# Fourier mixing and a two-layer network on one core: the last transform's copies with their two loops exchanged

## The chip, the cores and the metric

The kernel runs on one core of a Trainium2 chip. The metric is device time in microseconds of one execution. TensorE is written PE in the profile (its weight loads PEld), VectorE DVE, ScalarE ACT, GpSimd POOL; SP issues DMAs only.

## The reference

Eight sequences of 3008 rows with 256 channels go through a Fourier transform along the sequence, a complex 256 x 256 layer, a soft threshold, and the inverse transform. The 24064 rows that come out go through a network with 2048 hidden channels.

```python
X = np.fft.rfft(x, axis=1)                      # x: (8, 3008, 256)
Yr = Xr @ w_r - Xi @ w_i + b_r
Yi = Xr @ w_i + Xi @ w_r + b_i
Y  = soft(Yr, 0.01) + 1j * soft(Yi, 0.01)       # sign(v) * max(|v| - 0.01, 0)
y  = np.fft.irfft(Y, n=3008, axis=1).reshape(24064, 256)
h  = y @ w_in                                   # 256 -> 2048
out = (s * np.maximum(h, 0) ** 2 + b) @ w_out   # 2048 -> 256
```

## The kernel before

The transform of length 3008 is split into 94 x 32, with row n = 32 n1 + n2 (n1 below 94, n2 below 32), so that each part is a matmul with a small table. For every batch there are four steps. The first (`s1_units`) multiplies by the table of length 94. The second and third (`s23_units`) do the transform of length 32, the complex layer, the threshold and the transform back, with a turn through DRAM on either side. The last (`s4_units`) multiplies by the table `C_t` of length 94 and gives `yt`.

`yt` holds the rows of a batch for the network: 128 partitions are 128 channels, `DC` = 2 blocks of channels, then 96 x 32 two-byte values (n1 outside, n2 inside), so that n2 is contiguous and one n1 is a row of 64 bytes. The network reads `yt` as the moving side of its first matmuls, sixteen n1 with all n2 at a time (512 rows).

The last step goes over fourteen groups: n2 in steps of five (0, 5, ..., 25, then two from 30 on), and for each of these the two blocks of channels. For a group, PE does one matmul for each n2 with 94 columns, one behind the other in a bank of PSUM (pool `psf`, two banks), so that in the bank n2 is outside and n1 inside, four bytes a value. Then `leave_bank` (its copy is at L297) puts down one copy of 470 values (188 for the last groups) per partition that turns the order round and writes fp16 into `yt`.

Whether a copy runs on ACT or DVE, and in which place, is not decided while the program is built: `later` collects such pieces, and the table `TURNS` gives every piece its engine and its place in the order, written out by hand. The order on PE is in the program too: for each block of 128 hidden channels (a slot) come two matmuls of the first layer into one half of a double bank (`psh`, two of them), some matmuls of the second layer into `psa`, and a unit of the transform of a later batch. The fourteen units of the last step take the last slots before the batch's own tiles begin (for batch 1, sixteen slots around that point). A batch's first tile needs all its copies; for batch 1, whose tiles go over half the n2 at a time, the copies of that half.

Other work on ACT and DVE in these slots: relu (L1122 on ACT, L1124 on DVE) and square (L1133, L1135) of the hidden values, sums of squares for a product with seven instead of eight block products (L1276), and the sums that leave `psa` (L1234, L1333). POOL copies a batch's last 14 n1 from `yt` (L1036) once all copies are done, and issues DMAs behind that (x at L353, an adding DMA at L1290). Matmuls all appear at L234. Batch 0 has a last step of its own in `first_batch`, with groups of four n2.

Of the kernel before, what the change touches and what calls it, by code (L numbers as in the profile page):

```python
# [16 lines left out]
N1 = 94  # L17
# [140 lines left out]
def kernel(  # L158
# [73 lines left out]
    def matmul(out, lhs, rhs, **how):  # L232
        pump()
        return nc.tensor.matmul(out, lhs, rhs, **how)  # L234
# [37 lines left out]
    def need(ops):  # L272
        assert all(op.gone for op in ops)

    def later(emit, cost, needs=(), frees=None):

        op = SimpleNamespace(emit=emit, cost=cost, needs=list(needs), gone=False)
        if frees is not None:
            reads[id(frees)].append(op)
        if pe["on"]:  # L280
            pieces.append(op)
            return op
        e = min(cost)
        if "act" in cost:
            e = "act" if act_first(cost["act"], cost["dve"]) else "dve"
            work(e, cost[e])
        begin(op, e)
        return op
# [6 lines left out]
    def leave_bank(dst, bank, src, cols, needs=()):  # L295
        def emit(e):
            (nc.scalar.copy if e == "act" else nc.vector.tensor_copy)(out=dst, in_=src)  # L297

        return later(emit, copy_cost(cols), needs=needs, frees=bank)
# [30 lines left out]
    def one_bank():  # L330
        return track("psf", 2, fpool.tile([P, 512], F32, name="psf", tag="psf"))
# [672 lines left out]
    def s4_units(b):  # L1004

        groups = []
        for lo in range(0, N2, 5):
            for ec in range(DC):
                groups.append((lo, min(5, N2 - lo), ec))

        def unit(g):
            n2, w, ec = groups[g]
            if g == 0:
                yts[b] = ypool.tile([P, DC, 96, N2], F16, name="yt", tag="yt")
            yt = yts[b]
            ps = one_bank()
            need([half_loads[(b, h)] for h in {n2 // HW, (n2 + w - 1) // HW}])
            for j in range(w):
                h, k = divmod(n2 + j, HW)
                matmul(  # L1020
                    ps[:, j * N1 : (j + 1) * N1],
                    vs[(b, h)][:, k, ec * P : (ec + 1) * P], C_t[:, 0:N1],
                    start=True, stop=True,
                )

            done = leave_bank(
                yt[:, ec, 0:N1, n2 : n2 + w], ps,
                ps[:, 0 : w * N1].rearrange("p (j n) -> p n j", n=N1), w * N1,
            )
            y_ops[b].append((n2, w, done))  # L1030
            if g == len(groups) - 1 and b >= 2:
                pr, half = divmod(b, 2)
                if half == 0:
                    tails[pr] = tpool.tile([P, DC, 2, 14, N2], F16, name="tail", tag="tail")
                tail_copies[b] = later(
                    lambda e: nc.gpsimd.tensor_copy(  # L1036
                        out=tails[pr][:, :, half], in_=yt[:, :, 80:94, :]
                    ),
                    {"pool": 1.8}, needs=[op for _, _, op in y_ops[b]],
                )  # L1040

        return [lambda g=g: unit(g) for g in range(len(groups))]


# [419 lines left out]
    for b in range(2, B):  # L1464
        s0, s1, s2 = mark[b - 2], mark[b - 1], mark[b]
        p = s1 - s0
# [4 lines left out]
        p = s2 - s1  # L1471
# [57 lines left out]
```

## Time and profile before

| | |
|---|---|
| median of 3 runs | 835.43 us (834.75 to 836.34) |
| the profiled execution | 835.52 us |
| its span | 833.7 us |
| granted TensorE clock | 1.00 |
| last-step copies of batches 1 to 7 | 56 on ACT, 42 on DVE |
| stages of these copies, first copy to last | 93.67 us in seven pieces |

The profile is of one execution. A group row such as those in the prediction gives line, engine, operation, what is written and read, shape and count, then the busy time in us, the mean of one in ns, and the idle time of the engine before them with what ended it. A row of the timeline gives start and duration in us, and in brackets the engine's idle time before it. Neighbouring instructions of an engine overlap by about 0.1 us, so durations on a full engine add up to a little more than the time.

### The profile page before, as it was taken

What the parts mean: (1) busy time and instruction counts of PE and PEld (TensorE: products, weight loads), DVE (VectorE), ACT (ScalarE), POOL (GpSimd) and SP (SyncE); (2) the same over time, 40 slices, a digit from 0 to 9 for tenths busy, and PEclk for the clock granted to TensorE, in tenths of its full rate; (3) what the DMA queues carried; (4) which work ended last, traced back from release to release, by engine and by line L of the source; (5) the groups of instructions that cost most, each with busy time, mean ns of one, the idle gap of its engine ahead of it and who ended that gap; (6) DMA issues with size and microseconds to landing.
All of it is one profiled execution on the core that took longest, in us unless ns stands there. A gap on an engine that the chain in (4) does not pass through costs nothing.

```text
span 833.7 us, 19076 instructions
## 1 busy us (share of the span) xinstructions
PE 818.9 (98%) x7662; PEld 598.5 (72%) x7662; DVE 736.8 (88%) x1192; ACT 702.2 (84%) x874; POOL 83.4 (10%) x112
## 2 busy tenths in 40 slices
PE   7999999999999999999999999999999999999997
PEld 6857777777677767777677766777667777767765
DVE  5988989997898999998899979999989989889984
ACT  5989889989798889888889988897879987878774
POOL 4630000100011000110001100110001000001000
PEclk9999999999999999999999999999999999999999
DMA  8963546664547367454656545654566333513222
GB/s 202 182 170 82 120 138 171 131 129 123 173 114 166 85 176 188 108 118 128 176 141 161 112 124 150 150 130 116 129 177 149 72 92 96 140 45 77 74 49 77
DMA packets 114929, 107.14 MB, mean 129 GB/s; under 512 B 11036, under 2 KB 99104, under 8 KB 113496
## 3 DMA queue, kind: packets, MB, share of 16 engines
q1 hardware_dynamic: 100760, 80.55, 33.2%
q0 software_dynamic: 14080, 25.37, 18.5%
q8 instruction: 60, 0.98, 0.5%
q14 instruction: 29, 0.24, 0.1%
HBM read 53.52 MB, written 46.66 MB: 120 GB/s over the span
## 4 chain that ended last, share of the span: by engine, by line
PE 83%; DVE 8%; DMA 5%; ACT 2%; issue 1%; POOL 0%; SPq 0%; DVEq 0%; ACTq 0%; POOLq 0%
PE psh L234 34%; PE psa L234 31%; PE psf L234 17%; DMA ring<-ring 2%; DMA gt<-gt 2%; DVE rt L1124 1%; DMA x<-in_x_dram 1%; PE psm L234 1%; DVE gt L1135 1%; ACT rt L1122 1%; DVE u L297 1%; DVE yt L297 1%; DVE gt L1276 1%; DVE ring L934 0%; POOL x L370 0%
## 5 line engine op out<-in xcount | busy, mean ns | idle before, releaser
L234 PEld LDWEIGHTS <-gt 128*128 128x128 f16 (+1 forms) x3696 | 305.1, 101 | 168.9 <-DMA gt<-gt 1.1
L234 PE MATMUL psh<-yt,w_in 128*128 128x512 f16 (+1 forms) x1344 | 397.2, 378 | 1.5 <-ACT u L297 0.8
L1122 ACT ACTIVATE rt<-psh 128x1024 f32<-128x1024 f32 (+2 forms) x310 | 311.4, 1006 | 63.1 <-PE psh L234 55.7
L234 PE MATMUL psa<-w_out_t,gt 128*128 128x256 f16 (+3 forms) x2448 | 310.1, 253 | 0.7 <-DMA gt<-gt 0.6
L1133 ACT ACTIVATE gt<-rt 128x1024 f16<-128x1024 f32 (+2 forms) x254 | 261.6, 1041 | 11.4 <-DVE rt L1124 8.6
L1135 DVE TENSOR_TENSOR gt<-rt 128x1024 f16<-128x1024 f32 (+2 forms) x130 | 154.3, 1194 | 7.7 <-ACT rt L1122 7.0
L234 PEld LDWEIGHTS <-w_in 128*128 128x128 f16 x1536 | 136.3, 98 | 25.2 <-issue 3.2
L1124 DVE TENSOR_SCALAR rt<-psh 128x1024 f32<-128x1024 f32 (+2 forms) x74 | 88.2, 1193 | 19.9 <-PE psh L234 17.5
L1290 POOL DMA_DIRECT2D gt<-gt x42 | 38.1, 907 | 505.5 <-DVE gt L1276 231.6
L234 PE MATMUL psa<-T_s,gt 128*128 128x128 f16 (+1 forms) x944 | 79.6, 219 | 0.3 <-DVE zz L1333 0.3
L890 DVE TENSOR_TENSOR ring<-psf,s 128x512 f16<-128x512 f32 x84 | 57.6, 686 | 19.9 <-PE psf L234 11.1
L234 PE MATMUL psh<-tail,w_in 128*128 128x512 f16 (+1 forms) x192 | 52.1, 353 | 0.0
L234 PEld LDWEIGHTS <-xf 128*128 128x128 f16 x504 | 47.1, 98 | 4.9 <-DVE xf L850 0.5
L234 PE MATMUL psf<-W_g,xf 128*128 128x256 f16 x336 | 50.4, 273 | 0.0
L297 ACT CAST yt<-psf 128x470 f16<-128x470 f32 (+2 forms) x60 | 37.1, 646 | 4.4 <-PE psf L234 4.2
L1234 DVE SCALAR_TENSOR_TENSOR ost<-psa,s_bc,bias_bc 128x512 f32<-128x512 f32 (+2 forms) x51 | 36.9, 723 | 3.0 <-PE psa L234 2.9
L234 PE MATMUL psf<-x,A_t 94*96 94x512 f16 x102 | 38.9, 382 | 0.3 <-DVE u L297 0.2
L297 ACT CAST xf<-psf 128x512 f16<-128x512 f32 x52 | 30.3, 585 | 10.1 <-PE psf L234 9.9
L1333 DVE SCALAR_TENSOR_TENSOR ost<-psa,s_bc,zz 128x256 f32<-128x256 f32 (+1 forms) x80 | 36.6, 477 | 1.6 <-PE psa L234 0.8
L234 PE MATMUL psf<-C_t,vs 96*128 96x94 f16 (+1 forms) x484 | 37.7, 205 | 0.3 <-ACT yt L297 0.3
L297 ACT CAST u<-psf 96x512 f16<-96x512 f32 x54 | 31.0, 578 | 6.7 <-PE psf L234 5.4
L297 ACT CAST v<-psf 128x512 f16<-128x512 f32 x49 | 28.6, 583 | 9.3 <-PE psf L234 9.1
(121 smaller groups left out, 890.8 us busy)
## 6 DMA issues: line engine op xcount, KB each, us to landing
out_dram<-ost SPq DMA_DIRECT2D x65, 256.0 KB
ud<-u SPq DMA_DIRECT2D x56, 192.0 KB
us<-ud SPq DMA_DIRECT2D x28, 384.0 KB
vd<-v SPq DMA_DIRECT2D x42, 256.0 KB
vs<-vd SPq DMA_DIRECT2D x14, 768.0 KB
x<-in_x_dram POOLq DMA_DIRECT2D x28, 376.0 KB, 6.4
gt<-gt POOLq DMA_DIRECT2D x38, 256.0 KB, 4.0
ring<-ring SPq DMA_DIRECT2D x120, 64.0 KB
```

The lines of the kernel that those rows point to most:

```text
L234: return nc.tensor.matmul(out, lhs, rhs, **how)
L297: (nc.scalar.copy if e == "act" else nc.vector.tensor_copy)(out=dst, in_=src)
L890: lambda e: nc.vector.tensor_tensor(out=ring[0][:, i % 4], in0=ps, in1=hold[i // 2][:, i % 2].unsqueeze(1).to_broadcast([P, 2, D]), op=ALU ...
L1122: nc.scalar.activation(out=rt, in_=ps[:, :, 0:w], func=AF.Relu)
L1124: nc.vector.tensor_scalar(out=rt, in0=ps[:, :, 0:w], scalar1=0.0, scalar2=None, op0=ALU.max)
L1133: nc.scalar.activation(out=gt, in_=rr, func=AF.Square)
L1135: nc.vector.tensor_tensor(out=gt, in0=rr, in1=rr, op=ALU.mult)
L1234: nc.vector.scalar_tensor_tensor(out=osts[number % 3][0:size, 0:k], in0=ps[0:size, 0:k], scalar=s_bc[0:size], in1=bias_bc[0:size].unsqueez ...
L1276: nc.vector.tensor_tensor(out=out, in0=a, in1=b, op=op)
L1290: nc.gpsimd.dma_start(out=a12, in_=a11, accum_op=ALU.add)
L1333: nc.vector.scalar_tensor_tensor(out=out, in0=of, scalar=s_bc[0:size], in1=other, op0=ALU.mult, op1=ALU.add)
```

## The change

The copies of `s4_units` write the same values from the same bank to the same places, in the other order: n2 outside, n1 inside. The source is then read in the order in which it lies, and the destination gets one two-byte value in each 64-byte row before the next.

```diff
             done = leave_bank(
-                yt[:, ec, 0:N1, n2 : n2 + w], ps,
-                ps[:, 0 : w * N1].rearrange("p (j n) -> p n j", n=N1), w * N1,
+                yt[:, ec, 0:N1, n2 : n2 + w].rearrange("p n j -> p j n"), ps,
+                ps[:, 0 : w * N1].rearrange("p (j n) -> p j n", n=N1), w * N1,
             )
```

Batch 0's copies, the table of turns and all other lines are as before.

## The prediction

> **What bounds the kernel now.** I read the busy shares first, then the chain that ended last.
>
> ```profile
> PE 818.9 (98%) x7662; PEld 598.5 (72%) x7662; DVE 736.8 (88%) x1192; ACT 702.2 (84%) x874; POOL 83.4 (10%) x112
> PE 83%; DVE 8%; DMA 5%; ACT 2%; issue 1%; POOL 0%; SPq 0%; DVEq 0%; ACTq 0%; POOLq 0%
> ```
>
> TensorE (PE) sets the time. The copies run on ScalarE (ACT) and VectorE (DVE), which have slack on the whole. What counts is their slack in the seven stages in which the copies run: batches 1 to 7, from first copy to last. The busy time by stage is the second view (columns: window, its length, busy time of PE, PEld, DVE, ACT, POOL, then clock, DMA share and GB/s):
>
> ```profile
> 230.63:243.60 12.97, 12.97 (x181) 10.20 (x179) 12.14 (x22) 12.26 (x18) 1.76 (x2) 1.00 0.59 153
> 718.50:731.20 12.70, 12.69 (x186) 10.69 (x185) 11.11 (x19) 12.67 (x20) 1.71 (x2) 1.00 0.31 65
> sum 93.67, PE 93.29 PEld 73.73 DVE 88.93 ACT 89.79 POOL 12.07; mean PE 13.33 PEld 10.53 DVE 12.70 ACT 12.83 POOL 1.72
> ```
>
> In these 93.67 us PE idles 0.38, ACT 3.88 and DVE 4.74: half a microsecond per stage and engine. Three engines are full at once, so more work on ACT or DVE is not hidden here.
>
> The groups by shape, for the price of a copy today:
>
> ```profile
> L297 ACT CAST yt<-psf 128x470 f16<-128x470 f32 x52 | 34.0, 683 | 2.9 <-PE psf L234 2.7
> L297 DVE CAST yt<-psf 128x470 f16<-128x470 f32 x32 | 22.4, 704 | 3.4 <-PE psf L234 3.4
> L297 ACT CAST yt<-psf 128x188 f16<-128x188 f32 x4 | 1.2, 321 | 0.0
> L297 DVE CAST yt<-psf 128x188 f16<-128x188 f32 x10 | 3.2, 347 | 1.1 <-PE psf L234 1.0
> L297 ACT CAST v<-psf 128x512 f16<-128x512 f32 x49 | 28.6, 583 | 9.3 <-PE psf L234 9.1
> L297 DVE CAST v<-psf 128x512 f16<-128x512 f32 x35 | 23.8, 681 | 2.0 <-PE psf L234 1.9
> ```
>
> The v rows read and write in order. With the 128x1024 rows at L1122 and L1124 (1022 and 1219 ns), a value costs (1022 - 583)/512 = 0.857 ns on ACT and 1.051 on DVE, over a fixed 144 and 143 ns. At that rate 470 values take 547 (ACT) and 637 ns (DVE), and 188 take 305 and 340.
>
> The yt copies lie above that, and single instructions show where. In batch 2 the first copies start at n2 = 0, 0, 5, 5, 10, ...:
>
> ```profile
> 230.63 0.55 ACT L297 CAST yt<-psf 128x470 f16<-128x470 f32 x1
> 232.07 0.83 ACT L297 CAST yt<-psf 128x470 f16<-128x470 f32 x1
> 239.12 0.75 ACT L297 CAST yt<-psf 128x470 f16<-128x470 f32 x1 [0.17 <-PE psf L234]
> ```
> ```profile
> 231.06 0.65 DVE L297 CAST yt<-psf 128x470 f16<-128x470 f32 x1 [0.40 <-PE psf L234]
> 236.17 0.74 DVE L297 CAST yt<-psf 128x470 f16<-128x470 f32 x1
> 240.19 0.64 DVE L297 CAST yt<-psf 128x470 f16<-128x470 f32 x1
> ```
>
> The means over the seven stages, by starting n2, read instruction by instruction: at 0, 10 and 25, ACT 585 and DVE 645 ns; at 15 and 20, ACT 762 and DVE 738; at 5, ACT 828 and DVE 818. PSUM is read the same way in all of them. What differs is the place of the written run: five two-byte values, ten bytes, in a 64-byte row of yt. Runs at 0, 10 and 25 lie within one aligned block of 16 bytes; at 15 and 20 one value is cut off from four; at 5 the cut is 3 + 2. So the write side has a price by block, and the strided PSUM read has next to none (645 against 637). After the change every value is written 64 bytes from the last, a block each.
>
> **The change part by part.** No instruction is added, moved or reordered: the order of all engines stays, with 52 + 4 copies on ACT and 32 + 10 on DVE in these stages (470 and 188 values). Batch 0 keeps its own copies. Only the price changes, and no row shows single values at a 64-byte step. The bounds:
> - Nothing: 547/305 ns on ACT, 637/340 on DVE (470/188 values). ACT loses 7.1 us in all, DVE 2.2.
> - The pair price. The 188-value copies write two values per 64-byte row, at (321 - 144)/94 = 1.88 ns a row on ACT and (347 - 143)/94 = 2.17 on DVE. If a single value needs as long as such a pair: ACT 144 + 470 x 1.88 = 1.03 us (0.50 for 188), DVE 1.16 (0.55).
> - The price of the cut-off value. The runs cut 1 + 4 pay (762 - 585)/94 = 1.88 ns extra on ACT and (738 - 645)/94 = 0.99 on DVE per lone value. On all values: ACT 585 + 470 x 1.88 = 1.47 us (0.68), DVE 1.11 (0.53).
> - The price of the 3 + 2 cut (243/94 = 2.59 and 173/94 = 1.84 ns) on every value: ACT 1.80 us (0.81), DVE 1.51 (0.69).
>
> The pair rows have the right step, the cut rows the right number of values. On DVE both say the same: I take 1.13 us (0.54). On ACT I take the middle, 1.25 (0.59).
>
> The Trainium skill, "Vector Engine (DVE) Microarchitecture Reference", section "5.2 Measured stream behaviour on trn2", speaks against this change: a destination that hops with every element is given as 1.71 ns an element for far hops and 2.50 for a 96-byte step, against 1.05 for runs of two or more. An estimate by that page is 0.95 to 1.32 us for 470 values on DVE, and with the same prices on ACT some 6 to 28 us for the kernel by the same sum as below. "SBUF — State Buffer", "Specifications (TRN2)", says that a 16-byte line needs two hits for full bandwidth; the 3 + 2 runs have two or more on each line and still cost 818 ns, so the trace agrees with the line and not with the count.
>
> Now the path. Stage by stage, the extra work of an engine is the new price less what its copies take now. What hides it is the engine's idle time in the stage, and the lead of the last copy over the first matmul that reads it. Where units and copies end in batch 2:
>
> ```profile
> 242.62 0.25 PE L234 MATMUL psf<-C_t,vs 96*128 96x94 f16 x2
> 244.30 0.59 PE L234 MATMUL psh<-yt,w_in 128*128 128x512 f16 x2
> ```
>
> The last copy ends at 243.59 and the matmul at 244.30 waits for all copies of its batch: a lead of 0.71. For batches 3 to 7 the leads are 0.95, 0.56, 0.70, 0.54 and 0.62. Batch 1 reads its second half later; there I allow 1.0, the time between two units on the two psf banks. Extra on ACT at 1.25 us, batches 1 to 7: 4.3, 4.0, 5.1, 3.9, 5.4, 3.0, 4.9 (sum 30.6); on DVE 2.3, 2.5, 1.8, 2.5, 1.5, 3.3, 1.7 (15.6). ACT is the later engine in all but batch 6, where DVE has eight of the fourteen copies. Idle on ACT: 0.20, 0.71, 0.34, 0.65, 1.32, 0.63, 0.03; on DVE in batch 6: 0.14. Take idle and lead off the later engine: 3.1 + 2.6 + 3.8 + 2.7 + 3.4 + 2.6 + 4.2 = 22.3 us. PE has nothing to catch this up with: 0.38 us idle.
>
> What queues behind: on ACT the relus at L1122 and squares at L1133, whose two psh banks hold up PE's next pair; on DVE the sums at L1276 and the out additions, which free psa. On POOL the tail copy waits for the last yt copy (26.8 us in all today), and behind it the gt additions and x loads. They shift with PE, and I count nothing more for them.
>
> The profiled execution took 835.52 us (span 833.7), the median of the runs is 835.43. So 835.4 + 22.3 = 857.7 us.
>
> **The rivals.**
> - *Pair price on both engines.* For it: the 188-value rows have this very step and run at full rate. Against: a lone value may not go like a pair. The same sum with ACT 1.03 and DVE 1.16: 1.5 + 1.2 + 1.8 + 1.3 + 1.4 + 2.8 + 2.2 = 12.2 us, giving 847.6.
> - *Cut-off price on every value.* For it: lone values exist in the trace and cost that. The sum is 33.4 us, giving 868.8; with the 3 + 2 price 51.7, giving 887.1. Against: those runs go to the neighbouring block, and ours never do.
> - *The hop is free* (ends at no change or faster). If the cost lies in cutting a run, not in the block, then writes at 64 bytes are free, as for pairs, and the cuts are gone: ACT 7.1 us and DVE 2.2 less. PE can take up only its 0.38 us of idle time in the stages, and perhaps as much at their ends: 834.7 to 835.1. It decides while an ACT copy stays under about 0.84 us (3.88 idle + 5.08 lead over 56 copies is 0.16 above 683) and a DVE copy under about 0.94. The Trainium skill's "Advanced Engine Details and Errata", "PSUM Cachelines", wants every two consecutive elements adjacent, by which the read in order would gain; the trace shows 8 ns of 645 to be had. That nothing changes because the pattern is folded back is in this case too: the order of the loops in the built instructions does change (94x5 to 5x94).
>
> **How the numbers follow.** Middle price 0.32, pair price 0.27, cut-off price 0.20, 3 + 2 price or worse 0.08, free or unchanged 0.13. The range leaves out the free case and the 3 + 2 price: from 842, the pair case with some more lead, to 872, the cut-off case with a little on top. A difference under 0.2% (1.7 us) can't be told from none. The free case is mostly within it: 0.10 same and 0.03 faster. The rest, 0.87, is slower.
>
> **What would show it.** Right: the 470-value copies near 1.25 us on ACT and 1.13 on DVE, alike for all starting n2; stages 2 to 4 us longer, with PE idle before psh matmuls, on yt or on ACT's relus; nothing else changed. Wrong: copies at about 0.55 and 0.64 us (free), or ACT copies above 1.45; or copies as forecast but stages longer by less than 1 us, so that leads are larger than I counted; or stages longer by ACT and DVE together, so that the two delays add.

## The result, and the profile after

The changed kernel takes 921.93 us (median; 920.77 to 923.95) against 835.8 us in the same comparison: a ratio of 1.1035, 95% interval 1.1012 to 1.1058, or +86 us. Forecast were +22 us and a range that ended at 872. The direction and the place were right; the price of a copy was not.

The busy time of the page, then three of the seven stages of the copies (the second, the sixth and the seventh, first copy to last) and the sum of all seven:

```profile
PE 845.2 (92%) x7662; PEld 612.9 (67%) x7662; DVE 790.6 (86%) x1192; ACT 782.6 (85%) x874; POOL 83.3 (9%) x112
243.40:268.90 25.50, 18.04 (x189) 12.98 (x187) 20.64 (x21) 23.61 (x19) 1.76 (x2) 0.87 0.29 75
683.00:707.30 24.30, 15.70 (x193) 11.19 (x190) 24.23 (x24) 21.96 (x18) 1.77 (x2) 1.00 0.36 92
790.50:817.90 27.40, 17.44 (x194) 13.42 (x192) 16.97 (x20) 27.36 (x22) 1.71 (x2) 0.88 0.14 30
sum 182.30, PE 121.22 PEld 88.52 DVE 144.15 ACT 173.40 POOL 12.06; mean PE 17.32 PEld 12.65 DVE 20.59 ACT 24.77 POOL 1.72
```

The seven stages grew from 93.67 to 182.30 us, by 88.6. The rest of the span went from 740.0 to 737.8. So the whole loss lies where the copies are, and there ACT is now busy for 173.4 of 182.3 us while PE is not. The groups of the copies:

```profile
L297 ACT CAST yt<-psf 128x470 f16<-128x470 f32 x52 | 114.2, 2338 | 6.4 <-PE psf L234 6.4
L297 DVE CAST yt<-psf 128x470 f16<-128x470 f32 x32 | 71.4, 2256 | 26.9 <-PE psf L234 26.9
L297 ACT CAST yt<-psf 128x188 f16<-128x188 f32 x4 | 3.8, 1080 | 1.8 <-PE psf L234 1.8
L297 DVE CAST yt<-psf 128x188 f16<-128x188 f32 x10 | 10.0, 1074 | 6.3 <-PE psf L234 6.3
L297 ACT CAST v<-psf 128x512 f16<-128x512 f32 x49 | 28.5, 582 | 8.2 <-PE psf L234 7.9
L297 DVE CAST v<-psf 128x512 f16<-128x512 f32 x35 | 23.9, 682 | 2.0 <-PE psf L234 1.8
```

A copy of 470 values went from 0.68 to 2.34 us on ACT and from 0.70 to 2.26 on DVE. The v copies, which write in order, are as before. The two engines, whose rates differ (0.857 and 1.051 ns a value), now pay nearly the same: (2256 - 1074)/282 = 4.2 ns a value on DVE and 4.5 on ACT. So what limits them now is not the engine's own rate.

How PE comes to wait, in the waits of the whole kernel (waiting line, who ends the wait, total us, times, longest) and in the timeline of batch 2, ACT first, then one line of PE:

```profile
PE psf L234 <- ACT yt L297: 48.7, 43, 1.9
PE psf L234 <- DVE yt L297: 10.5, 13, 1.6
```
```profile
243.35 2.23 ACT L297 CAST yt<-psf 128x470 f16<-128x470 f32 x1
245.09 1.29 ACT L1122 ACTIVATE rt<-psh 128x960 f32<-128x960 f32 x1
246.28 2.22 ACT L297 CAST yt<-psf 128x470 f16<-128x470 f32 x1
```
```profile
245.63 0.37 PE L234 MATMUL psf<-C_t,vs 96*128 96x94 f16 x5 [1.08 <-ACT yt L297]
```

PE can't write the next unit of the last step before a copy has left one of the two psf banks, and everything behind that matmul on PE waits too. The two waits come to 59.2 us; in the seven stages PE now idles 61.1 us (182.30 - 121.22) where it idled 0.38.

The relu behind a copy starts 0.5 us before the copy's end and then takes 1.29 us. In the kernel before, a relu of this shape took 0.97:

```profile
242.49 0.97 ACT L1122 ACTIVATE rt<-psh 128x960 f32<-128x960 f32 x1 [0.45 <-PE psh L234]
```

That would fit a relu whose own writes queue behind those of the copy, but no run shows this. The start is 0.4 us earlier than the usual overlap of 0.1 us would have it, and the relu is 0.32 us longer, so the two nearly cancel.

### The profile page after: what moved, and what is told of

The parts are those of the page before. It is cut to its first block, busy times and chain, and to the rows that moved or that the text cites. A ratio compares the mean times of both kernels' runs of the same rounds, so it can differ in the third digit from the quotient of the medians.

```text
span 920.1 us, 19076 instructions
## 1 busy us (share of the span) xinstructions
PE 845.2 (92%) x7662; PEld 612.9 (67%) x7662; DVE 790.6 (86%) x1192; ACT 782.6 (85%) x874; POOL 83.3 (9%) x112
## 5 line engine op out<-in xcount | busy, mean ns | idle before, releaser
L234 PEld LDWEIGHTS <-gt 128*128 128x128 f16 (+1 forms) x3696 | 309.4, 102 | 173.2 <-issue 7.1
L234 PE MATMUL psh<-yt,w_in 128*128 128x512 f16 (+1 forms) x1344 | 401.5, 381 | 3.2 <-ACT rt L1122 1.1
L1122 ACT ACTIVATE rt<-psh 128x1024 f32<-128x1024 f32 (+2 forms) x310 | 320.6, 1037 | 63.4 <-PE psh L234 58.0
L1133 ACT ACTIVATE gt<-rt 128x1024 f16<-128x1024 f32 (+2 forms) x254 | 265.9, 1059 | 12.5 <-DVE rt L1124 9.8
L297 ACT CAST yt<-psf 128x470 f16<-128x470 f32 (+2 forms) x60 | 120.0, 2131 | 9.7 <-PE psf L234 9.7
L297 DVE CAST yt<-psf 128x470 f16<-128x470 f32 (+2 forms) x47 | 83.4, 1823 | 33.2 <-PE psf L234 33.2
L1124 DVE TENSOR_SCALAR rt<-psh 128x1024 f32<-128x1024 f32 (+2 forms) x74 | 88.4, 1196 | 20.3 <-PE psh L234 17.8
L234 PE MATMUL psf<-C_t,vs 96*128 96x94 f16 (+1 forms) x484 | 40.8, 217 | 58.7 <-ACT yt L297 48.4
L234 PE MATMUL psa<-T_s,gt 128*128 128x128 f16 (+1 forms) x944 | 82.4, 224 | 0.5 <-DVE zz L1333 0.5
L234 PEld LDWEIGHTS <-vs 96*128 96x128 f16 x512 | 34.5, 104 | 66.7 <-issue 65.7
L234 PE MATMUL psh<-tail,w_in 128*128 128x512 f16 (+1 forms) x192 | 55.8, 374 | 0.5 <-ACT rt L1122 0.5
```

Source lines behind the costliest of these rows:

```text
L1122: nc.scalar.activation(out=rt, in_=ps[:, :, 0:w], func=AF.Relu)
L1124: nc.vector.tensor_scalar(out=rt, in0=ps[:, :, 0:w], scalar1=0.0, scalar2=None, op0=ALU.max)
L1133: nc.scalar.activation(out=gt, in_=rr, func=AF.Square)
```

## The experiments

Two theories on the price. **W**: a write of a single two-byte value to a place of its own costs, whichever engine does it. **R**: the order of the PSUM read costs. Two on the path: the later engine of a stage sets its time (**path**), or the delays of the two engines add up (**sum**).

**The copy by itself.** A small kernel that computes nothing of the reference: one bank per engine is filled once, then each form of the copy runs four times on ACT alone and four times on DVE alone, then both engines together. Its lines differ in the destination, some in the source too, for example:

```python
go(e, step(d16, e, 32), src(e))   # j outside at +1 element, n inside at 32 elements (64 bytes)
go(e, pairs(d16, e, 30), src_p(e))  # 235 pairs of neighbours, one pair per 64-byte row, from element 30
```

> The copy by itself: 470 values from one bank, four times each on ACT alone, then on DVE alone, with the written values at steps from 2 to 256 bytes; nothing else of the kernel is computed. In the changed kernel a copy took about 2.24 us on either engine. Theory W (the write of a single two-byte value to a new place is what costs, 4.4 ns whichever engine): 2.2 us at 64 bytes on both engines, from PSUM and from SBUF alike, and 0.55 (ACT) and 0.64 us (DVE) for a strided read with a contiguous write. Rival R (the read in order from PSUM costs): the contiguous write of an in-order read is slow, and the copy from SBUF is fast. Inside W three rivals: W-block, a new 16-byte block per value costs: steps of 16 bytes and more all near 2.2 us, 4 and 8 bytes clearly less. W-bank, a power-of-two step hits one bank: 66, 68, 72, 80 and 96 bytes well under 2.2 us, 128 and 256 as slow or slower. W-half, a write of less than a four-byte word has to be merged: fp32 values at 64 bytes near 0.6 us, fp16 pairs that fill a word too. Both engines at once: if the write side of the memory is shared, each copy takes about 4.4 us; if not, 2.2.

Measured in one execution, one copy of 470 values in ns. The first of four can be up to 0.34 us longer where the form before it was a slow one, so the rows give the typical one of the four:

| destination | ACT | DVE |
|---|---|---|
| contiguous, read in order | 550 | 647 |
| contiguous, read with a step of 376 bytes | 550 | 648 |
| step 4, 8, 16 bytes | 682, 1199, 2233 | 682, 1196, 2232 |
| step 32, 64, 66, 80, 96, 256 bytes | 2125, 2192, 2191, 2181, 2375, 2247 | 2123, 2193, 2191, 2180, 2373, 2246 |
| step 64 bytes, source in SBUF | 2226 | 2192 |
| fp32, step 64 and 80 bytes | 942, 1128 | 942, 1125 |
| pairs at 64 bytes, from an even place | 551 | 648 |
| pairs at 64 bytes, from an odd place in one block | 1177 | 1178 |
| pairs at 64 bytes, across two blocks of 16 bytes | 2117 | 2116 |

Five groups of it in the profile, taken by their times: single values at 64 bytes (ACT, DVE), pairs from an odd place (DVE) and from an even place (DVE, without the first), and two of the fp32 copies at 64 bytes (ACT). The mean in ns stands behind the busy time:

```profile
L76 ACT CAST da<-psa 128x470 f16<-128x470 f32 x4 | 8.8, 2192 | 0.1
L77 DVE CAST dv<-psv 128x470 f16<-128x470 f32 x4 | 8.8, 2193 | 0.1
L77 DVE CAST dv<-psv 128x470 f16<-128x470 f32 x4 | 4.7, 1178 | 0.1
L77 DVE CAST dv<-psv 128x470 f16<-128x470 f32 x3 | 1.9, 648 | 0.1
L76 ACT COPY fa<-psa 128x470 f32<-128x470 f32 x2 | 1.9, 942 | 0.1
```

R is out: with a strided read and a contiguous write the copy costs what it costs in order. W holds, and at 64 bytes the two engines agree to the nanosecond. Of its three forms, a bank struck by a power of two is out (66, 80 and 96 bytes are no cheaper). What is left is both others together: a block of 16 bytes costs about 4.4 ns when it gets part of a four-byte word (470 x 4.4 + 144 = 2212 against 2123 to 2375 measured; at 8 bytes a step 235 blocks, 1178; at 4 bytes 118 blocks, 663). The two rows of pairs within one block are the clearest sign: 235 blocks in either, whole words at 551 ns, half words at 1177. fp32 values, which are whole words, cost (942 - 144)/470 = 1.7 ns at the same 64 bytes and 2.1 at 80; that is far below 4.4, but a copy takes 0.94 us and not the 0.6 that were expected.

With both engines at once a 64-byte copy took 2268 ns on each instead of 2192 (2236 to 2427 when the small kernel of the next study did the same), and 2197 beside a plain copy on the other engine. A shared limit would have given about 4.4 us; what was seen is 2 to 11% more. The law gives 2.21 us for a copy of the change; why it took 2.34 on ACT and 2.26 on DVE in the kernel is not shown, but both lie within what the two engines took together.

**Runs of one to eight values at each place in a row.** The same small kernel with 94 runs a copy (58 for runs of eight).

> Again the copy by itself, four times on each engine alone: 94 runs (58 or 78 of the long ones) of one to eight values, at every place in a 64-byte row. From the first study: theory H (a 16-byte block that gets a half word, that is two bytes of a four-byte word, takes 4.4 ns, whichever engine; a block that gets whole words only takes at most 1.7). By H: one value at place 0 or 1, 94 x 4.4 + 144 = 560 ns; two at 0, 305 to 340 ns; two at 1, 560; four at 0 or 2, the rate of the engine (466 and 538); four at 1 or 3 (a half word at either end), 560 in one block; two at 7 (a half word in either of two blocks), 970. The runs of five at 0 to 3, one block with one half word: 570 and 650; at 4, 6 and 7 (a block of whole words and one with a half word): 730; at 5: 817 as seen. The whole 470 in a row but one value off: 59 blocks of whole words, full speed (550 and 640), unless the engine sends pairs and cuts them: then 59 x 4.4 is hidden too. fp32 runs have no half words: 94 singles 305 to 340 ns, fives at the engine's rate. Rival S (it is the step: any value at a place of its own costs, whatever its width): the fp32 singles as dear as the fp16 singles, four at 1 no dearer than four at 0. On 64 partitions: 2.19 us as on 128, if each partition has its own writes.

| run of, at place | ACT | DVE | half words in |
|---|---|---|---|
| 1 at 0; 3 at 0; 4 at 1 | 568; 569; 570 | 566; 566; 568 | one block |
| 2 at 0; 4 at 0; 4 at 2 | 318; 473; 473 | 353; 549; 549 | none |
| 2 at 7; 4 at 5 | 943; 945 | 941; 944 | two blocks |
| 5 at 0 to 3 | 570 | 649 | one block |
| 5 at 4 or 7 | 736 | 733 | one of two blocks |
| 5 at 5 or 6 | 818 | 816 | one of two blocks |
| 8 at 1 (58 runs) | 775 | 774 | two blocks |
| 94 fp32 singles; 94 fp32 runs of 5 at 0 | 317; 632 | 315; 649 | none |
| 470 in a row, from place 0; from place 1 | 552; 555 | 647; 649 | none; the two ends |

Theory H gives most rows within 30 ns, but not three of them. A run of five at 5 or 6, also with half words in one block of its two, costs 82 ns more than at 4 or 7 (for place 6, 730 were expected). Eight at 1 should take 58 x 2 x 4.4 + 144 = 654 ns and takes 775. Runs of five fp32 values, whole words only, were expected at the engine's rate (547 ns on ACT) and take 632 there, so whole words over two blocks are not always hidden. Why is open for all three. Rival S (the step alone) is out: singles in fp32 cost 317 ns where fp16 ones cost 568. On 64 partitions the 64-byte copy takes 2187 ns on ACT, as on 128.

**One engine at a time.** The exchange only where ACT, or only where DVE, does the copy:

```diff
-            (nc.scalar.copy if e == "act" else nc.vector.tensor_copy)(out=dst, in_=src)
+            d, s = [a.rearrange("p n j -> p j n") if e in flip else a for a in (dst, src)]
+            (nc.scalar.copy if e == "act" else nc.vector.tensor_copy)(out=d, in_=s)
 ...                                 # and in s4_units, at the call of leave_bank:
+                flip=("act",),      # or: ("dve",)
```

> The loops are exchanged only where ACT does the copy (52 + 4 of 98), DVE keeps the old form. Path theory (in each stage the engine that is later sets the time; its extra work less its idle time and the lead): ACT's extra is 52 x 1.66 + 4 x 0.76 = 89 us by the durations of the changed kernel, less 3.9 idle and 5.1 lead, so about +80 us (916); if the next instruction's overlap with the copy's end is taken off, 1.4 us a copy and +66 (902). Rival (the delays of the two engines add up to the +86): ACT's share by its part of the extra work, 89 of 146 us, so +53 (889).

> The loops are exchanged only where DVE does the copy (32 + 10 of 98), ACT keeps the old form. Path theory: DVE's extra 57 us less 4.7 idle and 5.1 lead, so about +47 us (883), and with the ACT kernel more than the +86 of both together, since the delays lie side by side. Rival (they add up): 57 of 146 us, +34 (870).

On ACT alone 912.97 us, ratio 1.0932 (1.0916 to 1.0948), +78. On DVE alone 882.58 us, 1.0571 (1.0546 to 1.0597), +48. Together they would be +126, and the change as a whole is +86: the delays lie side by side. The groups of the DVE kernel, and PE's wait for DVE's copies in it:

```profile
L298 DVE CAST yt<-psf 128x470 f16<-128x470 f32 x32 | 70.4, 2259 | 2.2 <-PE psf L234 2.2
L298 ACT CAST yt<-psf 128x470 f16<-128x470 f32 x52 | 34.8, 677 | 22.7 <-PE psf L234 22.5
PE psf L234 <- DVE yt L298: 33.4, 32, 1.8
```

ACT now has 22.7 us idle before its own copies, waiting for PE, which waits 33.4 us for DVE. The path sum, with each kernel's own copy times in place of the forecast ones and the idle times and leads of before, gives 84.0 us for the change (span +86.3), 78.7 for ACT alone (+77.7) and 47.3 for DVE alone (+45.2).

**Whole words in the exchanged order, and the same values singly.** Each group copies only four of its five n2, from an even place; the other six n2 of a batch (4, 5, 14, 15, 24, 25) are left out and set to zero by POOL. One kernel writes pairs, n1 between them, the other single values as in the change:

```diff
+            at = n2 % 2
+            m = w // 2 * 2
+            dst = yt[:, ec, 0:N1, n2 + at : n2 + at + m]
+            src = ps[:, at * N1 : (at + m) * N1]
             done = leave_bank(
-                yt[:, ec, 0:N1, n2 : n2 + w], ps,
-                ps[:, 0 : w * N1].rearrange("p (j n) -> p n j", n=N1), w * N1,
+                dst.rearrange("p n (a b) -> p a n b", b=2), ps,          # or: "p n j -> p j n"
+                src.rearrange("p (a b n) -> p a n b", b=2, n=N1), w * N1,  # or: "p (j n) -> p j n"
```

> The kernel with n2 outside and n1 inside as in the change, but the values go in whole words: pairs of n2 outside, n1, then the two of a pair. To have only whole words it leaves out one n2 of each group of five (n2 = 4, 5, 14, 15, 24, 25; these are set to zero by POOL), so a copy has 376 values. Theory H (half words cost): 144 + 376 x 0.857 = 0.47 us on ACT and 0.54 on DVE, less than the 0.68 and 0.70 of the kernel before, and since PE is the bound there, the same time, 834 to 836 us. Rival S (the step, or the order of the loops, costs): each value or pair at 64 bytes costs 4.4 ns, 0.97 us for 188 pairs, or 1.78 us if it is per value: +8 to +50 us.

> The same values as in the kernel that goes by pairs, 376 a copy (the same six n2 left out), but one at a time, in the order of the change. Theory H and S alike: 376 x 4.4 + 144 = 1.78 us a copy on both engines, 0.98 for the last groups. The path sum gives ACT 52 x 1.10 + 4 x 0.66 = 60 us extra, less 3.9 idle and 5.1 lead, with DVE the later engine in batch 6: +50 to +55 us (887).

By pairs 833.66 us, ratio 0.9989 (0.9979 to 0.9999); singly 896.92 us, 1.0735 (1.0719 to 1.0751), +62. The same places are written with the same 64-byte step, and the groups are a factor of 3.4 to 4 apart (pairs first, then singles):

```profile
L297 ACT CAST yt<-psf 128x376 f16<-128x376 f32 x52 | 25.0, 487 | 6.5 <-PE psf L234 6.2
L297 DVE CAST yt<-psf 128x376 f16<-128x376 f32 x32 | 17.5, 546 | 4.6 <-PE psf L234 4.1
```
```profile
L297 ACT CAST yt<-psf 128x376 f16<-128x376 f32 x52 | 92.9, 1924 | 3.3 <-PE psf L234 3.3
L297 DVE CAST yt<-psf 128x376 f16<-128x376 f32 x32 | 58.1, 1845 | 19.6 <-PE psf L234 19.4
```

The pairs go into half as many blocks, which alone would explain a factor of two. So neither n2 outside nor the step of 64 bytes costs in the kernel; the half words do. The singles were dearer than the 1.78 us expected, 1.85 to 1.92, and with these times the path sum gives 61.8 us.

**What a stage can hide.** The exchange for the first two of the fourteen copies only, and for the last two only:

```diff
+                flip=("act", "dve") if n2 == 0 else (),   # or: n2 == 30
```

> The loops are exchanged only for n2 = 0 to 4, the first two of the fourteen copies of a batch (9 on ACT, 5 on DVE in all). Path theory: the extra is 9 x 1.74 = 15.7 us on ACT and 5 x 1.63 = 8 on DVE, stage by stage 1.6 to 3.5 on the later engine, of which idle time and lead hide 0.6 to 2.0: about +7 us (843). Rival (PE waits for the bank behind every slow copy, before idle time later in the stage can be used): little is hidden, +12 to +15 us (849).

> The loops are exchanged only for n2 = 30 and 31, the last two of a batch's fourteen copies (4 on ACT, 10 on DVE; 0.32 to 0.35 us before, 0.98 after). Path sum with all the idle time of the stage: 1.3 us more on one engine in most batches, of which idle time and lead (0.5 to 1.0) hide nearly all: +0 to +2 us (836). Rival (idle time that lies before the slow copies is of no use, only the lead of the last copy counts): 1.3 less 0.6 in six batches, +3 to +5 us (839).

The first two: 851.97 us, 1.0197 (1.0180 to 1.0214), +17. The last two: 839.70 us, 1.0053 (1.0036 to 1.0070), +4.6. The second came out with the rival, the first above it. With their own copy times the path sum gives 11.8 and 1.0 us, where the spans of the profiled executions grew by 17.1 and 2.7. So in these two kernels the path sum takes off too much idle time and lead. That idle time before a slow copy is of no use to it, and that behind it only in part, would fit both kernels, but no run separates the two. It is a few us in all, and small beside the +86.

**Fewer half words in the old order.** All values are copied, n1 outside, but the groups of n2 start elsewhere:

```diff
-        for lo in range(0, N2, 5):
+        for lo, w in ((0, 4), (4, 5), (9, 5), (14, 4), (18, 5), (23, 5), (28, 4)):
```

> The loops as before the change (n1 outside, the run of n2 inside), all values copied, but the seven groups of n2 start at 0, 4, 9, 14, 18, 23, 28 with 4, 5, 5, 4, 5, 5 and 4 of them, so that fewer blocks get half words. By the copies measured alone (ns on ACT): 473 + 734 + 570 + 474 + 570 + 734 + 473 = 4028 for one block of channels, against 570 + 817 + 570 + 734 + 737 + 570 + 318 = 4316 with the groups of the kernel before: 0.6 us less work in each stage, 4 us in all over both engines. Theory (PE is the bound before, ACT and DVE have what they need): no change within 0.2%, 834 to 836 us. Rival (the stages wait for the copies already before the change): up to 4 us less, 831.

834.56 us, ratio 0.9992 (0.9982 to 1.0002): no change that can be told. By means and counts the copies of batches 1 to 7 took 59.6 us instead of 62.8, so 3.2 of the expected 4 us were saved. Here cheaper copies brought nothing, since PE already set the time.

## Why the prediction was wrong

- **What bounds the kernel, and where the change bites: right.** PE outside, three full engines in the seven stages. The stages took all of the loss, and the outside none.
- **The path sum: right for a change of this size.** It takes idle time and lead off the later engine, stage by stage. With the measured copies it gives 84.0 of 86.3 us. In the kernel with its first two copies exchanged it takes off too much (11.8 of 17.1 us); of the 86 us here that would be a small part. ACT was the later engine in all stages but the sixth, as forecast; there DVE is busy for 24.2 of 24.3 us.
- **The price of a copy: wrong, and this is the step that failed.** Taken were 1.25 us on ACT and 1.13 on DVE; measured 2.34 and 2.26. What the runs showed in its place: every single value puts half a word into a block of 16 bytes of its own, and that takes 4.2 to 4.5 ns on either engine. Even the dearest rival, the 3 + 2 cut on every value (1.80 and 1.51, left out of the range with a chance of 0.08), was too low. Three readings led there. First, the pair rows were taken for the price of a write at this step. But 1.88 and 2.17 ns a row is little more than the engine's own time for two values (2 x 0.857 and 2 x 1.051), and two values at n2 = 30 are one whole word, whose write (1.7 ns alone in fp32 at 64 bytes) hides behind that. Second, the cost of a cut was read as the extra over a run that isn't cut. But a run that isn't cut has a half word too: its block takes 4.4 ns, and the engine needs 5 x 0.857 = 4.3 ns (ACT) for five values anyway, so that the price stood there, hidden. It showed a little: the runs at 0, 10 and 25 took 585 ns on ACT where the rate gave 547. Third, one engine's extra was put on that engine's rate, so ACT and DVE got different prices per value, when the totals per run were nearly the same on both: by the prediction's own means (762 - 144)/94 = 6.6 and (738 - 143)/94 = 6.3 ns for 1 + 4, 7.3 and 7.2 for 3 + 2. That was a sign that the engines' own rates were not the limit.
- **The strided PSUM read costs next to nothing: right** (550 against 550 ns on ACT, 647 against 648 on DVE).
- **The free rival: wrong for single two-byte values.** Writes at 64 bytes hide behind the engine's own time only as fp16 pairs that fill a word. That the read in order would gain is not borne out by any run here.
- **The estimate from the page: too low for two-byte values.** The Trainium skill, "Vector Engine (DVE) Microarchitecture Reference", "5.2 Measured stream behaviour on trn2", gives 1.71 to 2.50 ns an element for hopping destinations, measured with four-byte streams. Here fp32 values take 1.7 ns at 64 bytes and 2.1 at 80, on both engines, so the trace agrees for whole words; fp16 values take 4.4, so the estimate carried that figure over to a case that it does not cover. The Trainium skill, "SBUF — State Buffer", "Specifications (TRN2)", asks for two hits on a 16-byte line for full bandwidth. The block of 16 bytes is in the runs too, but the count does not describe fp16 (three values at 0, one line, 569 ns; two at 0, one line, 318).

One thing was not the cause. The granted clock fell to 0.87 to 0.93 in six of the stages. In the sixth it stayed at 1.00, and that stage too grew, by 10.5 us. In the kernel that writes 376 values singly it was 1.00 in five stages, the second among them, which grew from 12.97 to 22.10 us. The sixth stage before, and the second of that kernel:

```profile
621.60:635.40 13.80, 13.80 (x186) 10.56 (x184) 13.66 (x24) 13.17 (x17) 1.77 (x2) 1.00 0.64 162
240.90:263.00 22.10, 15.52 (x189) 11.08 (x186) 18.54 (x21) 21.70 (x19) 1.76 (x2) 1.00 0.33 85
```

## What to carry to other kernels

When a copy writes two-byte values with a step, count the 16-byte blocks that get part of a four-byte word and take 4.4 ns for each as a first estimate; let innermost runs start at an even element and have an even length, as the pairs here, which at 64 bytes cost no more than in one piece (551 against 550 ns on ACT). A price read off a row is only the part that sticks out over the engine's own time: before it is used as a bound, ask what that row already hides. Compare two engines on the same work; where they take equal times although their rates differ, the limit is not their rate.

## What was not expected of the hardware

- A block of 16 bytes that gets half a word costs about 4.4 ns on ACT and DVE alike, four to five values' time; a single whole word 1.7 ns at a step of 64 bytes and 2.1 at 80. 470 fp16 values one position off in one run are not slowed (555 against 552 ns on ACT).
- The engines slow each other only a little in this: 2236 to 2427 ns with both at it, 2192 alone.
- The instruction behind such a copy on ACT starts about 0.5 us before the copy ends, and is lengthened by 0.3 us (L1122, 0.97 to 1.29).
